# Eight strided loads of 16 partitions for the first keys of a decode attention, instead of one of 16 and one of 112

## The chip, the cores and the metric

The kernel runs on one core of one Trainium2 chip. The metric is the device time of one execution in microseconds (us), the median over the runs; less is better.

## What is computed

One step of grouped-query attention for one sequence. There are 32 query heads with one query row each, and 8 key/value heads of 65536 rows of 128 bf16 numbers, so four query heads share the keys and values of one head. Keys and values together are 268.4 MB, and each is read once.

```python
B, Hq, Hkv, Sq, Sk, D = 1, 32, 8, 1, 65536, 128
k = jnp.repeat(k, Hq // Hkv, axis=1)
v = jnp.repeat(v, Hq // Hkv, axis=1)
scores = jnp.einsum("bhqd,bhkd->bhqk", q, k) * D ** -0.5
p = _softmax(scores, axis=-1)
return jnp.einsum("bhqk,bhkd->bhqd", p, v)
```

## The kernel before

The rows of a head are split in two halves (`pairs`, line 445), which makes 16 rounds (`NR`). In a round each of the 128 partitions holds 256 key rows and 256 value rows of one half, one after another as they lie in memory: 64 KB of keys for each partition, 8 MB for all, and as much of the values. A key row of all partitions together is a tile of 128 x 128. In memory, one partition's run begins 64 KB after that of the partition before.

Each round does this:

- TensorE transposes the key tiles, eight to a PSUM buffer (`pe_transposes`, line 132, the transposes at line 140). VectorE and ScalarE copy the buffers to `ktb` (`evict`, lines 235 and 237). TensorE multiplies the transposed tiles with the four queries (`pe_scores`, line 158).
- VectorE and GpSimd find the maximum, ScalarE takes the exponentials (line 405), and TensorE multiplies them with the values (`stretch`, line 184), which VectorE adds to the running output.

All key and value loads are issued by SP's queue in the order that is written out by hand in `sync_engine` (line 449). Keys lie in `kbuf`, which has room for 256 + 96 tiles, values in `vbuf`, which has room for 256. Loads of the next round wait until the buffers are free (`kfree`, set after the transposes of the first 160 tiles; `vfree` and `vmid`, set by the value products).

The first round's keys come in parts, so that TensorE can begin before all are there: tiles 0 to 63 (`K_PARTS[1]` is 64; 16 KB for each partition, 2 MB), 64 to 159, and 160 to 255 (24 KB for each partition each). The semaphores `krdy[0]` to `krdy[2]` tell that a part has landed, and `pe_transposes` waits for the right one ahead of the first tile of each part. The first part is cut once more, by partitions: 16 rows of partitions, which raise `kfirst` (line 478), and 112, which raise `krdy[0]` (line 479). TensorE waits for `kfirst` before it enters its loop (line 218), and for `krdy[0]` at the loop's first transposes. After the first part come the second and third part (line 462) and the values of the round (line 467), all of which are issued without a wait.

The last round's values come in pieces of 160, 62, 22, 9 and 3 tiles (`V_PIECES` for the last four), so that few products are left when the last one lands.

A DMA raises its semaphore by 16 in all; so seven loads that raise the same semaphore bring it to 7 * 16.

Of the kernel before, what the change touches and what calls it, by code (L numbers as in the profile page):

```python
# [10 lines left out]
P = 128  # L11
# [3 lines left out]
C = 96  # L15
A = 2 * T - C
K_PARTS = (0, 64, A)
# [24 lines left out]
def take(e, sem, n=1):  # L42

    e.wait_ge(sem, n)
    e.sem_inc(sem, -n)  # L45


def bass_standalone__gqa_softmax__decode_kernel(nc, q, k, v, out):
    _, Hq, _, D = q.shape
# [13 lines left out]
    def row_tile(odd, x):  # L63
        return (x + C) % (2 * T) if odd else x
# [6 lines left out]
    def sb(name, shape, dt):  # L71
        return S(nc.sbuf_tensor(name, shape, dt))

    def sem(name):
        return S(nc.semaphore(name))

    kbuf = sb("kbuf", [P, (2 * T + C) * D], DT.bfloat16)
# [38 lines left out]
    krdy = [sem(f"krdy{i}") for i in range(len(K_PARTS))]  # L116
    kfirst = sem("kfirst")
# [47 lines left out]
    def pe_keys(pe, i):  # L165
        for j in range(GA + LAG):
            if j < GA:
                pe_transposes(pe, j, C + j * TB)
            if j >= LAG:
                pe_scores(pe, j - LAG)  # L170
        with pe.If(i % 2 > 0):
            for j in range(GA, G):
                pe_transposes(pe, j, j * TB - A)
        with pe.If(i % 2 < 1):
            for j in range(GA, G):
                pe_transposes(pe, j, C + j * TB)
        for j in range(GA, G):
            pe_scores(pe, j)
# [11 lines left out]
    def pe_values(pe, i):  # L190

        take(pe, vrdy[0], 16)
        take(pe, exd)
        stretch(pe, 1).then_inc(vmid, 1)


        with pe.Fori(i % 2, 2) as s:
            with pe.If(s > 0):  # L200
                take(pe, vrdy[1], 16)
                take(pe, exd)
                stretch(pe, 2).then_inc(pvd, 1)
            with pe.If((i + s) % 2 < 1):
                take(pe, exd)
                stretch(pe, 0).then_inc(pvd, 1)

    def pe_last(pe):
        ins = pe.transpose(fin[0:R, 0:P], acc, identf[:, :])  # L209
        ins.wait_op(t_acc, 1, "sem-ge")  # L210
        ins.then_inc(s_fin, 1)

    def tensor_engine(pe):
        pe.wait_ge(q_sem, 16)
        pe.wait_ge(t_id, 1)
        pe.transpose(trb[0][:, 0:HR], qsb[:, :], ident[0:HR, 0:HR]).then_inc(s_x, 1)  # L216
        pe.wait_ge(t_qT, 1)
        pe.wait_ge(kfirst, 16)
        pe.addr_align(256, offset=LOOP_SLOT, max_nops=16)
        with pe.Fori(0, NR) as i:  # L220
            pe_keys(pe, i)
            pe_values(pe, i)
        pe_last(pe)
# [221 lines left out]
    def pairs(x):  # L445

        return x.rearrange("h (c p t) d -> (h c) p (t d)", c=HALVES, p=P)

    def sync_engine(e):
        kp, vp = pairs(kf), pairs(vf)  # L450

        def cols(a, b):
            return slice(a * D, b * D)

        def load_k(i, odd, split=(0,)):

            for n, f in enumerate(split):
                last = (split + (len(K_PARTS),))[n + 1]
                a, b = K_PARTS[f], (K_PARTS + (2 * T,))[last]
                r = row_tile(odd, a) if b - a < 2 * T else 0  # L460
                t = r if odd else C + r
                e.dma_start(kbuf[:, cols(t, t + b - a)], kp[i][:, cols(r, r + b - a)]).then_inc(krdy[f], 16)
                for x in range(f + 1, last):
                    e.sem_inc(krdy[x], 16)

        def load_v(i, ready, a, b):
            e.dma_start(vbuf[:, cols(a, b)], vp[i][:, cols(a, b)]).then_inc(ready, 16)

        def load_both(i, odd):
            take(e, kfree)  # L470
            load_k(i, odd)
            take(e, vfree)
            load_v(i, vrdy[0], 0, 2 * T)
            e.sem_inc(vrdy[1], 16)


        first = K_PARTS[1] * D
        e.dma_start(kbuf[0:16, C * D:C * D + first], kp[0][0:16, 0:first]).then_inc(kfirst, 16)
        e.dma_start(kbuf[16:P, C * D:C * D + first], kp[0][16:P, 0:first]).then_inc(krdy[0], 16)
        load_k(0, 0, (1, 2))  # L480
        load_v(0, vrdy[0], 0, 2 * T)

        for sm in [vrdy[1]] + vpiece:
            e.sem_inc(sm, 16)

        take(e, kfree)
        load_k(1, 1)
        e.wait_ge(vmid, 1)
        load_v(1, vrdy[0], C, A)
        take(e, vfree)  # L490
        e.sem_inc(vpiece[0], -16)
        load_v(1, vrdy[1], A, 2 * T)
        load_v(1, vpiece[0], 0, C)
        with e.Fori(1, H - 1) as h:
            load_both(2 * h, 0)
            load_both(2 * h + 1, 1)
        i = NR - 2
        take(e, kfree)
        load_k(i, 0, (0, 2))
        take(e, vfree)  # L500
        load_v(i, vrdy[0], 0, A)
        load_v(i, vrdy[1], A, 2 * T)
        i = NR - 1
        take(e, kfree)
        load_k(i, 1, (0, 1, 2))
        take(e, vfree)
        for sm in vpiece:
            e.sem_inc(sm, -16)
        load_v(i, vrdy[0], C, 2 * T)
        e.sem_inc(vrdy[1], 16)  # L510
        r = 0
        for n, sm in zip(V_PIECES, vpiece):
            load_v(i, sm, r, r + n)
            r += n
        ins = e.dma_start(of[HR - R:HR, :], olast[:, :])
        ins.wait_op(t_last, 1, "sem-ge")
        ins.then_inc(o_sem, 16)
        e.wait_ge(o_sem, 32)

    block = S(nc.Block())  # L520
    block.tensor(tensor_engine)
    block.vector(vector_engine)
    block.scalar(scalar_engine)
    block.gpsimd(gpsimd_engine)
    block.sync(sync_engine)
    es.close()

# [26 lines left out]
```

## Time and profile before

| | before |
|---|---|
| median of 3 runs | 633.45 us (633.38 to 633.49) |
| the profiled execution | 633.33 us |
| its span, from the first to the last instruction | 631.3 us |
| mean granted clock of TensorE | 0.77 |
| busy: TensorE, VectorE, ScalarE | 78%, 45%, 37% |
| moved by the DMA engines | 268.59 MB, mean 425 GB/s |

The profile's page divides the span into 40 slices of 15.8 us. A digit of an engine's row is its busy share in tenths; the DMA row has the mean busy share of the core's 16 DMA engines, the row below what they moved. Lines such as `L462` are lines of the kernel's file. A DMA's time to landing is counted from its issue to its semaphore. In rows of a timeline the columns are start, duration, engine, line, operation, output and input, and in brackets the idle time before it with what ended it. SPq is SP's queue of issues; PEq is TensorE's sequencer.

### The profile page before, as it was taken

What the parts mean: (1) busy time and instruction counts of PE and PEld (TensorE: products, weight loads), DVE (VectorE), ACT (ScalarE), POOL (GpSimd) and SP (SyncE); (2) the same over time, 40 slices, a digit from 0 to 9 for tenths busy, and PEclk for the clock granted to TensorE, in tenths of its full rate; (3) what the DMA queues carried; (4) which work ended last, traced back from release to release, by engine and by line L of the source; (5) the groups of instructions that cost most, each with busy time, mean ns of one, the idle gap of its engine ahead of it and who ended that gap; (6) DMA issues with size and microseconds to landing.
All of it is one profiled execution on the core that took longest, in us unless ns stands there. A gap on an engine that the chain in (4) does not pass through costs nothing. (4 is left out here: it accounts for less than half of the span.)

```text
span 631.3 us, 26949 instructions
## 1 busy us (share of the span) xinstructions
PE 489.3 (78%) x12290; PEld 484.8 (77%) x12290; DVE 284.4 (45%) x667; ACT 235.2 (37%) x466; POOL 16.4 (3%) x49
## 2 busy tenths in 40 slices
PE   2763994958959599596986949769596796999887
PEld 2763994958959499595986949769496796989886
DVE  2430562715527155361653616445172452747354
ACT  1330351523516144152442504436052351535343
POOL 0000000000000000000000000000000000000000
PEclk9875795967959587585876958779596785969696
DMA  9999999999999999999999999999999999999997
GB/s 279 446 446 410 415 446 448 419 444 419 444 436 432 432 432 436 432 432 436 432 432 432 432 440 424 444 424 444 424 444 432 436 432 432 412 433 426 432 433 293
DMA packets 6459, 268.59 MB, mean 425 GB/s; under 512 B 818, under 2 KB 946, under 8 KB 1202
## 3 DMA queue, kind: packets, MB, share of 16 engines
q1 hardware_dynamic: 6360, 268.44, 99.1%
q8 instruction: 7, 0.11, 0.1%
q10 hardware_dynamic: 90, 0.02, 0.0%
q14 instruction: 2, 0.02, 0.0%
HBM read 268.44 MB, written 0.01 MB: 425 GB/s over the span
## 5 line engine op out<-in xcount | busy, mean ns | idle before, releaser
L140 PE MATMUL trb<-ident,kbuf 128*128 128x128 bf16 x4096 | 302.2, 236 | 112.2 <-PEq L45 106.3
L140 PEld LDWEIGHTS trb<-ident,kbuf 128*128 128x128 bf16 x4096 | 269.9, 107 | 113.9 <-issue 113.5
L235 ACT ACTIVATE ktb<-trb 128x1024 bf16<-128x1024 bf16 x176 | 180.1, 1023 | 353.9 <-PE trb L140 347.4
L237 DVE COPY ktb<-trb 128x1024 bf16<-128x1024 bf16 x336 | 221.8, 689 | 173.8 <-PE trb L140 171.0
L158 PE MATMUL qkb<-qcur,ktb 128*128 128x4 bf16 x4096 | 132.3, 164 | 0.9 <-issue 0.9
L158 PEld LDWEIGHTS qkb<-qcur,ktb 128*128 128x128 bf16 x4096 | 124.5, 96 | 1.0 <-issue 1.0
L184 PE MATMUL pvb<-pts,vbuf 128*128 128x4 bf16 x2560 | 71.7, 166 | 13.4 <-PEq L45 9.7
L184 PEld LDWEIGHTS pvb<-pts,vbuf 128*128 128x128 bf16 x2560 | 69.9, 102 | 15.2 <-issue 14.8
L405 ACT ACTIVATE pts<-qkb,negm 128x160 bf16<-128x160 f32 (+1 forms) x128 | 51.9, 548 | 0.0
L184 PE MATMUL qkb<-pts,vbuf 128*128 128x4 bf16 x1536 | 43.4, 166 | 7.9 <-PEq L45 7.8
L184 PEld LDWEIGHTS qkb<-pts,vbuf 128*128 128x128 bf16 x1536 | 42.4, 104 | 8.5 <-issue 8.3
L272 DVE TENSOR_REDUCE cmax<-qkb 128x4 f32<-128x640 f32 (+1 forms) x32 | 22.1, 691 | 59.1 <-DVEq L45 59.1
L405 ACT ACTIVATION_READ_ACCUMULATOR pts<-qkb,negm 128x1 f32 x128 | 34.2, 267 | 0.0
L441 POOL PARTITION_ALL_REDUCE cmaxa<-cmax x32 | 12.0, 375 | 580.2 <-POOLq L45 580.2
L322 DVE COPY acc<-qkb 128x4 f32<-128x4 f32 x8 | 1.3, 162 | 40.9 <-DVEq L45 40.9
L399 ACT ACTIVATE alpha<-dm 128x4 f32<-128x4 f32 x32 | 6.4, 201 | 32.5 <-ACTq L45 32.5
L300 DVE TENSOR_TENSOR lp<-lp,alpha 128x4 f32<-128x4 f32 x24 | 3.9, 163 | 26.9 <-DVEq L45 26.9
L311 DVE TENSOR_TENSOR acc<-acc,pvb 128x4 f32<-128x4 f32 x32 | 5.0, 158 | 21.0 <-DVEq L45 20.1
L289 DVE TENSOR_TENSOR m<-m,cmaxa 128x4 f32<-128x4 f32 x24 | 3.8, 159 | 8.8 <-DVEq L45 8.8
L308 DVE TENSOR_TENSOR acc<-acc,alpha 128x4 f32<-128x4 f32 x24 | 3.9, 163 | 4.2 <-DVEq L45 3.7
L216 PE MATMUL trb<-ident,qsb 32*128 32x32 bf16 x1 | 0.2, 204 | 5.5 <-DMA qsb<-in_q_dram 5.5
L216 PEld LDWEIGHTS trb<-ident,qsb 32*128 32x128 bf16 x1 | 0.1, 100 | 5.5 <-DMA qsb<-in_q_dram 5.5
(42 smaller groups left out, 37.6 us busy)
## 6 DMA issues: line engine op xcount, KB each, us to landing
kbuf<-in_k_dram SPq DMA_DIRECT2D x5, 3072.0 KB, 25.2
vbuf<-in_v_dram SPq DMA_DIRECT2D x2, 5120.0 KB, 23.6
vbuf<-in_v_dram SPq DMA_DIRECT2D x3, 3072.0 KB, 20.1
kbuf<-in_k_dram SPq DMA_DIRECT2D x1, 5120.0 KB, 17.8
vbuf<-in_v_dram SPq DMA_DIRECT2D x1, 2048.0 KB, 18.2
kbuf<-in_k_dram SPq DMA_DIRECT2D x1, 2048.0 KB, 18.3
vbuf<-in_v_dram SPq DMA_DIRECT2D x1, 1984.0 KB, 31.3
kbuf<-in_k_dram SPq DMA_DIRECT2D x1, 1792.0 KB, 10.7
```

The costliest lines, as they stand in the source:

```text
L140: ins = pe.transpose(trb[j % NTB][:, i * P:(i + 1) * P], kbuf[:, t * D:(t + 1) * D], ident[:, :])
L158: ins = pe.matmul(bank[:, t * R:(t + 1) * R], lhsT=ktb[:, off:off + P], rhs=qcur[:, :], start=True, stop=True)
L184: ins = pe.matmul(vsum[q], lhsT=vbuf[:, r * D:(r + 1) * D], rhs=pts[:, r * R:(r + 1) * R], start=r == a, stop=r == b - 1)
L235: ins = e.activation(dst, trb[j % NTB][:, :], AF.Copy).then_inc(eva, 1)
L237: ins = e.tensor_copy(dst, trb[j % NTB][:, :]).then_inc(evd, 1)
L272: e.tensor_reduce(cmax[:, :], qkb[part][:, 0:n * R].rearrange("p (t g) -> p g t", g=R), AX.X, ALU.max).then_inc(cm, 1)
L300: chain(e, lambda: e.tensor_tensor(lp[:, :], lp[:, :], alpha[u % 2][:, :], ALU.mult), lambda: e.tensor_tensor(lp[:, :], lp[:, :], rsum[u % ...
L308: return lambda: e.tensor_tensor(acc, acc, alpha[u % 2][:, :], ALU.mult)
L311: return lambda: e.tensor_tensor(acc, acc, vsum[q], ALU.add)
L399: e.activation(alpha[u % 2][:, :], dm[u % 2][:, :], AF.Exp, scale=scale)
L405: ins = e.activation(pv[:, g, r:r + n], sv[:, g, 0:n], AF.Exp, bias=negm[b][:, g:g + 1], scale=scale, accum_out=rsum[b][:, g:g + 1])
L441: e.partition_all_reduce(cmaxa[:, :], cmax[:, :], P, bass.bass_isa.ReduceOp.max).then_inc(cma, 1)
```

## The change

The 128 rows of partitions of the first part were loaded as rows 0 to 15 and rows 16 to 127. Now they are eight loads of 16 rows each, and load p takes the rows p, p + 8, ... p + 120. The first seven raise `kfirst`, the eighth raises `krdy[0]`. TensorE waits for all of the first seven at `kfirst`, where before it waited for one load. The bytes, the source and the destination of each row are the same as before, and the eight loads stand where the two stood, ahead of everything else on SP's queue. The size of each run in memory (16 KB) is the same too. No other instruction of any engine is added, removed or moved.

```diff
@@ tensor_engine
         pe.wait_ge(t_qT, 1)
-        pe.wait_ge(kfirst, 16)
+        pe.wait_ge(kfirst, 7 * 16)
         pe.addr_align(256, offset=LOOP_SLOT, max_nops=16)
         with pe.Fori(0, NR) as i:
             pe_keys(pe, i)
@@ sync_engine
-        first = K_PARTS[1] * D
-        e.dma_start(kbuf[0:16, C * D:C * D + first], kp[0][0:16, 0:first]).then_inc(kfirst, 16)
-        e.dma_start(kbuf[16:P, C * D:C * D + first], kp[0][16:P, 0:first]).then_inc(krdy[0], 16)
+        n = K_PARTS[1]
+        for p in range(8):
+            ins = e.dma_start(kbuf[p:P:8, cols(C, C + n)], kp[0][p:P:8, cols(0, n)])
+            ins.then_inc(kfirst if p < 7 else krdy[0], 16)
         load_k(0, 0, (1, 2))
         load_v(0, vrdy[0], 0, 2 * T)
```

## The prediction

> **What bounds the kernel now.** I read four views in this order: the page's slices and its DMA section, the chain that ended last, the DMA issues with their time to landing, and the first microseconds in stages and in order of time. The page first:
>
> ```profile
> span 631.3 us, 26949 instructions
> PE 489.3 (78%) x12290; PEld 484.8 (77%) x12290; DVE 284.4 (45%) x667; ACT 235.2 (37%) x466; POOL 16.4 (3%) x49
> ...
> DMA  9999999999999999999999999999999999999997
> GB/s 279 446 446 410 415 446 448 419 444 419 444 436 432 432 432 436 432 432 436 432 432 432 432 440 424 444 424 444 424 444 432 436 432 432 412 433 426 432 433 293
> ...
> q1 hardware_dynamic: 6360, 268.44, 99.1%
> ```
>
> No compute engine is above 78%. The DMA engines are busy in every slice, and all slices but the first and the last move 410 to 448 GB/s. So the kernel is one long stream of 268.44 MB on one queue (q1). A stream that never pauses ends earlier only by moving its bytes faster, and the slice that stands out for that is the first, at 279 GB/s. The chain shows whether the end follows the stream:
>
> ```profile
> 621.24 4.52 PE pvb L184 x160
> 625.77 2.45 PE qkb L184 x84
> 628.22 0.01 issue
> 628.23 0.49 PE qkb L184 x12
> ```
>
> These are the last value products. The issues of the loads they wait for, in order of time and by size (KB, then median us from issue to landing), stand here:
>
> ```profile
> 593.97 2.23 SPq L467 DMA_DIRECT2D vbuf<-in_v_dram  x5
> ```
>
> ```profile
> vbuf<-in_v_dram SPq DMA_DIRECT2D x1, 1984.0 KB, 31.3
> vbuf<-in_v_dram SPq DMA_DIRECT2D x1, 704.0 KB, 32.6
> vbuf<-in_v_dram SPq DMA_DIRECT2D x1, 288.0 KB, 32.9
> vbuf<-in_v_dram SPq DMA_DIRECT2D x1, 96.0 KB, 32.6
> ```
>
> Five issues in 2.23 us are 0.45 us each, so the four small ones start near 594.4, 594.9, 595.3 and 595.8 and land near 625.7, 627.5, 628.2 and 628.4. The 84 products begin at 625.77 and the last 12 at 628.23, each just as its piece lands. What delays the whole stream by a microsecond therefore delays the end by a microsecond.
>
> The first microseconds in stages (window and its length, busy time of each engine, TensorE clock, DMA share, GB/s):
>
> ```profile
> 0.00:1.80 1.80, 0.00 (x0) 0.00 (x0) 0.57 (x6) 0.60 (x1) 0.98 (x9) 1.00 0.08 18
> 1.80:4.60 2.80, 0.00 (x0) 0.00 (x0) 1.95 (x12) 0.89 (x2) 0.00 (x0) 1.00 1.09 179
> 4.60:10.20 5.60, 0.20 (x1) 0.10 (x1) 0.59 (x4) 0.00 (x0) 0.00 (x0) 1.00 1.01 281
> 10.20:12.00 1.80, 0.00 (x0) 0.00 (x0) 0.00 (x0) 0.00 (x0) 0.00 (x0) 1.00 1.11 410
> 12.00:620.00 608.00, 481.31 (x12032) 477.35 (x12032) 277.53 (x623) 232.15 (x455) 14.63 (x38) 0.77 1.00 432
> ```
>
> The DMA share is full from 1.8 us on while the rate is not: the engines have work and are slow at it. Full rate is 432 GB/s, which is 27 GB/s on each of the 16 engines. The first part of the keys is 128 rows (partitions) of 16 KB, eight rows for each engine. Call one row on each of the 16 engines, 262 KB together, a turn. At full rate a turn takes 262 / 432 = 0.607 us. Before the change the first turn is the load of 16 rows and seven turns are the load of 112. The window 1.8:4.6 moved 179 x 2.8 = 501 KB, about two turns; the window 4.6:10.2 moved 1574 KB, six turns of 0.93 us. Their loads and landings:
>
> ```profile
> kbuf<-in_k_dram SPq DMA_DIRECT2D x1, 256.0 KB, 4.5
> kbuf<-in_k_dram SPq DMA_DIRECT2D x1, 1792.0 KB, 10.7
> ```
>
> ```profile
> 0.73 0.40 SPq L478 DMA_DIRECT2D kbuf<-in_k_dram  x1
> 1.19 0.41 SPq L479 DMA_DIRECT2D kbuf<-in_k_dram  x1
> 1.65 0.90 SPq L462 DMA_DIRECT2D kbuf<-in_k_dram  x2
> 2.59 0.44 SPq L467 DMA_DIRECT2D vbuf<-in_v_dram  x1
> ```
>
> The 16 rows land at 0.73 + 4.5 = 5.2 us, the 112 rows at 1.19 + 10.7 = 11.9 us.
>
> **The rate of a turn, before and after.** This is the term that decides. The loads of 128 rows run at full rate, so there are 16 ways into the on-chip memory at 27 GB/s each, with eight of the 128 rows behind each. The first turn writes 16 neighbouring rows. Two turns took 2.8 us, and one of the later kind takes 0.93, which leaves 1.9 us, 3.1 times 0.607; since an engine reads ahead of its writes (the third turn is read from 4.6, before the first has landed at 5.2) this is a lower bound, and I take four times, 2.43 us. Four neighbouring rows then share one way, and a way holds two such groups of four. [...]
>
> After the change the rows of a turn are p, p+8, ... p+120. They touch 16 of the 32 groups of four, every second one. Whether these fall on 16 ways once or on 8 ways twice depends on how far apart the two groups of one way lie. Neighbouring groups are excluded, for 16 neighbouring rows would then have only two ways and need 4.9 us. An even distance (4, 8 or 16 groups, as a layout by address bits has it) puts the rows of each turn in pairs, and the turn takes 2 x 0.607 = 1.21 us; an odd distance gives 0.607. The trace of before does not show the distance. Bounds from its rows: 0.607 (loads of 128 rows) and 2.43 us (16 neighbours); the nearest row in spacing is 0.93 (7 apart), but with a step of 8 the collisions repeat in every turn instead of sliding, so I take 1.21.
>
> [...]
>
> **The sum.** The first load's landing is 4.5 us after its issue, of which 2.43 was the turn, so 2.1 us is the way there and back. After the change the last of the eight loads lands at 0.73 + 2.1 + 8 x 1.21 = 12.5 us instead of 11.9: +0.6 us for the first part, and for the whole stream behind it, since every engine writes its first-part rows before anything else.
>
> SP issues eight loads for two, at 0.45 us each. The three bigger loads behind them move from 1.65, 2.1 and 2.59 to about 4.4, 4.9 and 5.3 us. They are needed when the eighth turn is drained, near 11.6 us, or at 1.8 + 8 x 0.607 = 6.7 us at full rate, so the move costs nothing; without that cover it would cost 2.7 us. Each load of 16 rows starts 0.45 us after the last and needs 1.21, so the queue doesn't run dry. Six further completions are bounded below by 0, and above by the tail: loads of 288 and 96 KB landed about 0.7 and 0.2 us after their forerunners, which is their bytes at 432 GB/s. I take 0. [...]
>
> The wait on kfirst now ends with the seventh load, at about 12.5 - 1.2 = 11.3 us instead of 5.2. What is queued behind it on TensorE is the loop's entry and then the wait for the rest of the first part:
>
> ```profile
> 12.04 6.04 PE L140 MATMUL trb<-ident,kbuf 128*128 128x128 bf16 x64 [6.36 <-PEq L45]
> 20.65 0.27 PE L140 MATMUL trb<-ident,kbuf 128*128 128x128 bf16 x1 [2.56 <-PEq L45]
> ```
>
> TensorE began at 12.04 when the 112 rows were in. It will begin near 12.7. It has 1.2 us for the loop's entry, which no row prices; if that took up to 2 us more, the 2.56 us of idle time after the first 64 transposes, spent waiting for the second part, would take it up, and the stream doesn't wait for TensorE there:
>
> ```profile
> 29.77 0.33 SPq L462 DMA_DIRECT2D kbuf<-in_k_dram  x1
> ```
>
> That next issue waits for the keys' buffer. By then 2.8 MB were moved up to 12 us (from the windows) and 17.8 us x 432 GB/s = 7.7 MB after it, of 16.8 MB issued; 6.3 MB, or 14 us, were still queued. So 0.6 us here is free, and only the stream's own delay stays. The profiled execution took 633.33 us, 2.0 beyond its span, and lies 0.12 under the median of 633.45. With +0.6: 633.9 against the profiled execution, 634.1 against the median.
>
> **Rivals.**
>
> [...]
>
> *Faster: collisions don't repeat.* If the distance matters little, or one of a pair gets ahead and they stop meeting, a turn takes the 0.93 us of the 112 rows. Then 0.73 + 2.1 + 7.4 = 10.3 us, 1.6 us earlier: 631.9. For it speaks that this is the nearest measured row, and that the slow first turn, 2.43 us, is gone. [...]
>
> *Much faster: sixteen ways.* With an odd distance all turns run at 0.607: 7.7 us, 4.2 earlier, 629.3. Only the layout speaks against it.
>
> *The wait on kfirst becomes the bound:* it would need more than 1.2 + 2.5 us of loop entry and then 14 us of cushion; I give it nothing.
>
> **How the numbers follow.** A change of 0.2%, 1.27 us, is about what a measurement of this kernel can tell from none. Pairs that share (forecast): 0.62, from +0.4 to +1.7, since a loss of 10% on each turn is easily had; 0.43 of that lies within 1.27 us and 0.19 above. Pairs that cost more: 0.18. Turns of 0.93: 0.13. Full rate: 0.07. So faster 0.20, same 0.43, slower 0.37. The range leaves out the full-rate case and reaches to the middle of the costly pairs: 631.8 to 636.7. The forecast's own range is 633.8 to 635.1.
>
> **What would show it.** In the changed profile: window rates near 218 GB/s from about 2 to 11.5 us; the eighth load landing near 12.5 us; TensorE's first key transposes near 12.7, and its second stop (20.65) and the last value pieces later by the same 0.6; kfirst's move without effect. Rates of 280 or more in that stretch would prove me wrong towards faster, under 200 towards slower. If the first part moves one way and the end another, the step from stream to end is wrong.

## The result: slower by 0.91 us, and the profile after

| | before | after |
|---|---|---|
| median of 22 runs each | 633.36 us | 634.27 us |
| range of the runs | 632.9 to 633.66 | 634.04 to 634.39 |
| ratio, 95% interval | | 1.0015 (1.0008 to 1.0021) |
| the profiled execution, and its span | 633.33, 631.3 | 634.24, 632.4 |

The change costs 0.15% (0.08% to 0.21%). The first microseconds of the changed kernel in stages, cut as they were before the change:

```profile
0.00:1.80 1.80, 0.00 (x0) 0.00 (x0) 0.57 (x6) 0.63 (x1) 0.98 (x9) 1.00 0.01 1
1.80:4.60 2.80, 0.18 (x1) 0.10 (x1) 2.12 (x13) 0.85 (x2) 0.00 (x0) 1.00 1.13 265
4.60:10.20 5.60, 0.00 (x0) 0.00 (x0) 0.42 (x3) 0.00 (x0) 0.00 (x0) 1.00 0.96 202
10.20:12.00 1.80, 0.00 (x0) 0.00 (x0) 0.00 (x0) 0.00 (x0) 0.00 (x0) 1.00 1.17 278
12.00:620.00 608.00, 478.53 (x11963) 474.64 (x11964) 276.15 (x620) 230.12 (x446) 14.63 (x38) 0.77 1.00 432
```

The opening is faster (265 GB/s for 179), which fits that the slow turn of 16 neighbouring rows is gone. The long middle is slower (202 for 281), and from 12 us on both streams run at 432. Cut where six turns begin and end, the middle shows the time of a turn:

```profile
3.90:11.30 7.40, 0.00 (x0) 0.00 (x0) 0.87 (x7) 0.00 (x0) 0.00 (x0) 1.00 1.02 213
```

262 KB at 213 GB/s are 1.23 us. SP's issues and TensorE's work in order of time, after the change:

```profile
0.73 5.04 SPq L479 DMA_DIRECT2D kbuf<-in_k_dram  x8
5.81 1.05 SPq L462 DMA_DIRECT2D kbuf<-in_k_dram  x2
6.91 0.44 SPq L467 DMA_DIRECT2D vbuf<-in_v_dram  x1
...
13.15 6.40 PE L140 MATMUL trb<-ident,kbuf 128*128 128x128 bf16 x64 [9.55 <-PEq L45]
21.77 0.66 PE L140 MATMUL trb<-ident,kbuf 128*128 128x128 bf16 x8 [2.22 <-PEq L45]
```

An issue took 0.63 us and not 0.45, and in the first 1.8 us hardly a byte moved (1 GB/s for 18). TensorE begins at 13.15 instead of 12.04, and its next stop ends at 21.77 instead of 20.65. The chain that ended last:

```profile
622.39 4.48 PE pvb L184 x160
626.87 0.03 issue
626.90 2.96 PE qkb L184 x96
```

The last value products begin at 626.90 instead of 625.77. So 1.1 us are lost before the first transpose, and it stays 1.1 us to the end. The whole executions differ by 0.91, a little less, as what lies outside the span differs by 0.2 between these two.

### The profile page after: what moved, and what is told of

It is laid out like the page before. It is cut to its first block, busy times and chain, and to the rows that moved or that the text cites. A ratio compares the mean times of both kernels' runs of the same rounds, so it can differ in the third digit from the quotient of the medians.

```text
span 632.4 us, 26955 instructions
## 1 busy us (share of the span) xinstructions
PE 488.4 (77%) x12290; PEld 483.8 (76%) x12290; DVE 284.1 (45%) x667; ACT 235.2 (37%) x466; POOL 16.4 (3%) x49
## 5 line engine op out<-in xcount | busy, mean ns | idle before, releaser
L290 DVE TENSOR_TENSOR dm<-m 128x4 f32<-128x4 f32 x24 | 3.9, 163 | 0.8
L301 DVE TENSOR_TENSOR lp<-lp,rsum 128x4 f32<-128x4 f32 x24 | 3.9, 162 | 0.8
```

Source lines behind the costliest of these rows:

```text
L290: lambda: e.tensor_tensor(dm[u % 2][:, :], mo[:, :], mn[:, :], ALU.subtract),
```

## Experiments

Each kernel below is the changed one with one more edit, timed beside the kernel before on the same chip. Three dots mark lines of an edit or a view that are left out; where an edit changes the number of loads, the count that TensorE waits for at `kfirst` follows it. For each, three rows are shown: the rate in a window inside the first part (its length, engine busy times, clock, DMA share, GB/s), and, from the timeline, TensorE's first key transposes and its last 96 value products.

**One load of 128 rows.**

```diff
-        pe.wait_ge(kfirst, 7 * 16)
...
-        for p in range(8):
-            ins = e.dma_start(kbuf[p:P:8, cols(C, C + n)], kp[0][p:P:8, cols(0, n)])
-            ins.then_inc(kfirst if p < 7 else krdy[0], 16)
+        e.dma_start(kbuf[:, cols(C, C + n)], kp[0][:, cols(0, n)]).then_inc(krdy[0], 16)
```

> The first part as one load of 128 rows that raises krdy[0]; the wait on kfirst is left out, since nothing raises it. Theory of the ways (16 ways into the on-chip memory, rows that are written in the same turn on the same way share it): each engine has a way to itself, a turn takes 0.61 us, the part lands near 7.2 us instead of 11.9 (before) or 13.0 (after), and the end follows: 628.5 to 629.5 us. Rival A (the start of the stream is slow whatever the rows are, since queues and memory have to come up to speed): turns of 0.9 us and more, landing after 10 us, 631.5 us or more. Rival B (the stream is not what sets the end): landing early, time within 0.3 us of 633.4.

```profile
3.50:7.10 3.60, 0.20 (x1) 0.10 (x1) 1.25 (x9) 0.00 (x0) 0.00 (x0) 1.00 0.99 425
...
8.37 6.37 PE L140 MATMUL trb<-ident,kbuf 128*128 128x128 bf16 x64 [2.94 <-PEq L45]
...
622.14 2.93 PE L184 MATMUL qkb<-pts,vbuf 128*128 128x4 bf16 x96
```

629.54 us, 0.9942 of the kernel before (0.9929 to 0.9956). Full rate from the third turn on, 0.62 us each. So the slow turns were not a matter of coming up to speed: rival A falls, and so does B, for the end moved with the landing. A slow start of its own remains: in the first 3.6 us this kernel moved no more than the changed one (147 and 148 GB/s on average). The part came about 1 us later than expected (8.2 for 7.2), and the time lies just above the forecast range.

**Eight loads by columns.** Each has all 128 rows and eight of the 64 tiles.

```diff
+        n = K_PARTS[1] // 8
...
+            a = p * n
+            ins = e.dma_start(kbuf[:, cols(C + a, C + a + n)], kp[0][:, cols(a, a + n)])
```

> Eight loads again, 256 KB each, but each has all 128 rows and an eighth of their columns (2 KB for each row). Theory of the ways: no sharing, so as fast as one load of 128 rows but for the pace of the issues (0.45 to 0.63 us each for 0.61 us of bytes): landing at 7 to 8 us, 628.5 to 630 us. Rival C (what costs is that there are eight loads, by their issue, their completions or their fixed price): landing at 12 us or later, 634 us or more.

```profile
3.50:8.00 4.50, 0.11 (x1) 0.00 (x0) 1.25 (x9) 0.00 (x0) 0.00 (x0) 1.00 0.93 288
...
9.99 5.84 PE L140 MATMUL trb<-ident,kbuf 128*128 128x128 bf16 x64 [6.39 <-PEq L45]
...
624.11 2.92 PE L184 MATMUL qkb<-pts,vbuf 128*128 128x4 bf16 x96
```

630.93 us, 0.9964 (0.9951 to 0.9978): a miss by 0.9 us at the slow end, and far from rival C. Eight loads of the same 256 KB beat the kernel before. They cost 1.4 us over one load (630.93 for 629.54; in the profiled executions TensorE begins at 9.99 for 8.37); whether that is the number of loads or the rows of 2 KB isn't separated here.

**Stride of 4 in one half of the rows.**

```diff
+            a, b = p // 4 * 64 + p % 4, p // 4 * 64 + 64
+            ins = e.dma_start(kbuf[a:b:4, cols(C, C + n)], kp[0][a:b:4, cols(0, n)])
```

> Eight loads of 16 rows with a stride of 4 inside one half of the rows (0, 4, ... 60 and so on, then 64, 68, ... 124 and so on): 16 neighbouring groups of four rows. If the two groups of one way lie 8 groups (32 rows) apart, the 16 rows of a load meet in pairs on 8 ways as with the stride of 8: turns of 1.26 us, landing near 13.0, 634.0 to 634.6 us. If they lie 16 groups (64 rows) apart, each row has its own way: 0.61 us, landing near 7.5, 628.5 to 629.5 us. If they lie 4 groups apart, four rows meet: about 20 us and 642 us.

```profile
3.80:11.10 7.30, 0.00 (x0) 0.00 (x0) 0.97 (x8) 0.00 (x0) 0.00 (x0) 1.00 1.01 219
...
12.82 5.46 PE L140 MATMUL trb<-ident,kbuf 128*128 128x128 bf16 x64 [9.22 <-PEq L45]
...
626.51 2.92 PE L184 MATMUL qkb<-pts,vbuf 128*128 128x4 bf16 x96
```

633.91 us, 1.0011 (1.0002 to 1.002), 0.1 us under the forecast range. Turns of 1.20 us: rows 0 to 60 in steps of four meet in pairs. That rules out a distance of 64 rows (0.61 us). It doesn't rule out 16 rows, where the expectation is wrong: with two groups of four on a way, those 16 groups would meet in pairs too, and not four at a time. The 32 neighbouring rows further down decide that: paired at 16 rows they would reach four ways and need some 2.4 us a turn (four times 0.607), and they need 1.23. So of the three distances 32 rows are left.

**Sixteen neighbouring rows, eight times.**

```diff
+            a, b = 16 * p, 16 * p + 16
+            ins = e.dma_start(kbuf[a:b, cols(C, C + n)], kp[0][a:b, cols(0, n)])
```

> Eight loads of 16 neighbouring rows: 0 to 15, 16 to 31, and so on. Theory of the ways: four rows on each of four ways in every turn, 2.43 us to 2.6 us each, so the part lands at 21.5 to 23.5 us and the time is 643 to 645 us. Rival C (eight loads cost what eight loads cost, whichever rows): 634.3 us as after the change. Rival B (the stream does not set the end): within 0.3 us of 634.3.

```profile
4.70:17.00 12.30, 0.20 (x1) 0.10 (x1) 0.60 (x4) 0.00 (x0) 0.00 (x0) 1.00 1.02 128
...
19.54 5.98 PE L140 MATMUL trb<-ident,kbuf 128*128 128x128 bf16 x64 [13.48 <-PEq L45]
...
633.20 2.93 PE L184 MATMUL qkb<-pts,vbuf 128*128 128x4 bf16 x96
```

641.35 us, 1.0131 (1.0115 to 1.0146). The number of loads and their size are those of the change; which rows go together costs 7 us more, and rivals B and C fall. But a turn takes 2.05 us and not 2.43, so the time falls short of the forecast range. The next pair of experiments bears on why.

**Another order of the same loads.** The changed kernel once more, and the same with the order 0, 4, 1, 5, 2, 6, 3, 7.

```diff
-        for p in range(8):
+        for i in range(8):
+            p = i // 2 + i % 2 * 4
...
-            ins.then_inc(kfirst if p < 7 else krdy[0], 16)
+            ins.then_inc(kfirst if i < 7 else krdy[0], 16)
```

> The changed kernel once more, as the yardstick for the three kernels beside it: first part landed near 13.0 us, 634.0 to 634.6 us.

> The same eight strided loads in the order 0, 4, 1, 5, 2, 6, 3, 7, so that each turn uses the other eight ways than the turn before it. In step (both engines of a pair always on the same way together): nothing changes, turns of 1.26 us, landing 12.8 to 13.2 us, 634.0 to 634.6 us. With a lead (an engine that is ahead of its partner has the next way to itself until the partner comes, so each turn is shorter by the lead; in the order 0 to 7 that can happen at one turn only, the fifth): turns of 0.9 to 1.15 us, landing 10 to 12.2 us, 631.4 to 633.6 us. If the number of strided loads or their issue were what costs, the order would not matter: 634.0 to 634.6 us.

The reordered kernel:

```profile
3.80:10.20 6.40, 0.00 (x0) 0.00 (x0) 0.97 (x8) 0.00 (x0) 0.00 (x0) 1.00 1.01 246
...
12.01 5.94 PE L140 MATMUL trb<-ident,kbuf 128*128 128x128 bf16 x64 [8.41 <-PEq L45]
...
625.72 2.92 PE L184 MATMUL qkb<-pts,vbuf 128*128 128x4 bf16 x96
```

The yardstick repeated at 634.20 us (1.0014, 1.0005 to 1.0023), the reordered kernel took 633.13 (0.9998, 0.9989 to 1.0007). Nothing but the order differs, and 1.07 us are gone, about as much as the whole loss of the change: a turn takes 262 / 246 = 1.07 us. The number of loads, their size and the pace of their issue (eight in 5.04 us) are the same in both, so none of them makes this difference. Partners in step would take the same time in both orders. That an engine gains by its lead when the next turn uses other ways is the theory that forecast this; how large the leads are no row shows. By that theory the ways change at each turn in the sixteen neighbouring rows too, which fits the 2.05 us, but wasn't tried apart from it.

**Fewer loads with a step.** Four loads of 32 rows with a stride of 4, and two of 64 with a stride of 2. These are the lines that issue the loads.

```diff
+        for p in range(4):
+            ins = e.dma_start(kbuf[p:P:4, cols(C, C + n)], kp[0][p:P:4, cols(0, n)])
```

```diff
+        for p in range(2):
+            ins = e.dma_start(kbuf[p:P:2, cols(C, C + n)], kp[0][p:P:2, cols(0, n)])
```

> [...] In step: 634.0 to 634.6 us. With a lead: as the changed order of loads, or up to 0.3 us earlier for the earlier first byte: 631.2 to 633.6 us. If the number of loads cost: half of what eight cost over one load of 128 rows, near 632 us, with turns that are still 1.26 us.

> [...] Theory of the ways: landing 11.5 to 12.9 us, 633 to 634.4 us, though there are only two loads. If the number of loads cost: as one load of 128 rows or a little more, 629.5 to 630.5 us. If the stride itself delays the first byte (2.1 us in place of 1.8), it does so here too, with an issue of 0.6 us and more.

First the four loads, then the two:

```profile
3.90:7.80 3.90, 0.00 (x0) 0.00 (x0) 0.88 (x7) 0.00 (x0) 0.00 (x0) 1.00 1.02 397
...
9.24 5.99 PE L140 MATMUL trb<-ident,kbuf 128*128 128x128 bf16 x64 [5.64 <-PEq L45]
...
623.13 2.92 PE L184 MATMUL qkb<-pts,vbuf 128*128 128x4 bf16 x96
```

```profile
3.80:7.40 3.60, 0.00 (x0) 0.00 (x0) 0.96 (x8) 0.00 (x0) 0.00 (x0) 1.00 1.03 437
...
8.39 6.44 PE L140 MATMUL trb<-ident,kbuf 128*128 128x128 bf16 x64 [4.79 <-PEq L45]
...
622.11 2.98 PE L184 MATMUL qkb<-pts,vbuf 128*128 128x4 bf16 x96
```

630.82 us (0.9962, 0.9948 to 0.9975) and 629.86 us (0.9947, 0.9933 to 0.9961). Both forecasts of the theory of the ways fell: turns of 0.66 and 0.60 us where 1.2 was forecast for partners in step. They follow if each engine takes consecutive rows of a load, which puts rows 8 apart into a turn. The four loads would then write the same rows turn by turn as the reordered eight loads, which took 1.07 us. The two loads came out in the range of the rival that the number of loads costs; the four are 1.2 us faster than that rival has them. At this point two readings were open: the engines are dealt the rows in another way, so that a load that reaches all 16 ways gives one to each engine; or what decides is the number of rows in a load, or of loads.

**The same number of loads without a step.** Four loads of 32 neighbouring rows, whose edit is shown, and two of 64 in the same way.

```diff
+            a, b = 32 * p, 32 * p + 32
+            ins = e.dma_start(kbuf[a:b, cols(C, C + n)], kp[0][a:b, cols(0, n)])
```

> Four loads of 32 neighbouring rows (0 to 31, 32 to 63, and so on), beside the four loads of 32 rows with a stride of 4 that ran turns of 0.61 us and landed at 9.1 us. Number and size of the loads are the same, and the step between rows is 1 and not 4. Theory of the ways: 32 neighbouring rows reach 8 of the 16 ways, so two engines meet on each: turns of 1.05 to 1.26 us, landing 10.7 to 12.6 us, 632 to 634 us. If the number of rows in a load decides (16 are slow, 32 are not): turns of 0.61 us, landing 8.5 to 9.1 us, 630 to 631 us. With a step of 1 the issue should be back at 0.45 us and the first byte at 1.8.

> Two loads of 64 neighbouring rows, beside the two loads of 64 rows with a stride of 2 that landed at 8.3 us. Theory of the ways: 64 neighbouring rows reach no more than the 8 ways that 32 reach, since rows 32 apart share one: turns of 1.2 to 1.26 us, landing 11.5 to 12.6 us, 632.7 to 634 us. If the number of rows or of loads decides: 0.61 us, landing near 8.2 us, 629.5 to 630.2 us.

First the four loads, then the two:

```profile
3.60:11.00 7.40, 0.20 (x1) 0.10 (x1) 1.15 (x9) 0.00 (x0) 0.00 (x0) 1.00 1.02 213
...
13.14 5.29 PE L140 MATMUL trb<-ident,kbuf 128*128 128x128 bf16 x64 [6.88 <-PEq L45]
...
626.83 2.92 PE L184 MATMUL qkb<-pts,vbuf 128*128 128x4 bf16 x96
```

```profile
4.10:11.60 7.50, 0.00 (x0) 0.00 (x0) 0.70 (x6) 0.00 (x0) 0.00 (x0) 1.00 1.00 210
...
13.55 5.20 PE L140 MATMUL trb<-ident,kbuf 128*128 128x128 bf16 x64 [9.95 <-PEq L45]
...
627.20 2.98 PE L184 MATMUL qkb<-pts,vbuf 128*128 128x4 bf16 x96
```

634.38 us (1.0018, 1.0009 to 1.0028) and 634.74 us (1.0024, 1.0015 to 1.0034), some 0.4 to 0.7 us above the forecast ranges. Turns of 1.23 and 1.25 us, with as many rows and loads as the two kernels of 0.66 and 0.60. So neither the number of rows in a load nor that of loads decides; which rows go together does, and pairs at 32 rows account for all four kernels. 64 neighbouring rows are no faster than 32 (1.25 us a turn for 1.23), as the theory of the ways forecast.

What no run separates is where the ways lie. Row r of every load here goes to partition r and comes from r x 64 KB further on in memory, so a way into the on-chip memory and a way out of the memory that holds the keys would look alike. That there are 16 of them (432 GB/s over 16 engines, and loads of 128 rows at that rate), and that they lead into the on-chip memory, is argued, not shown.

**The load of the queries moved.** In these traces the slow issues of 0.6 us went together with an early landing of the queries (1.6 to 1.8 us after their issue; with the fast issues 4.4 to 5.3, and 2.4 in the eight loads by columns), so the queries' load, on ACT's queue, was issued 0.45 us later: in the changed kernel, and in that of two loads of 64 rows.

```diff
-        e.dma_start(qsb[:, :], qf).then_inc(q_sem, 16)
         e.wait_ge(t_z, 1)
+        e.dma_start(qsb[:, :], qf).then_inc(q_sem, 16)
```

> The changed kernel, with the load of the queries on ACT's queue moved behind ACT's wait for GpSimd's memsets (about 0.5 us later), so that it doesn't start together with SP's first load. In the kernels so far the first byte of the keys came at 2.1 us, the queries landed 1.6 to 1.8 us after their issue and SP needed 0.6 us for each issue, or the first byte came at 1.8, the queries landed after 4.4 to 5.3 us and SP needed 0.45 us; never a mixture but for one (2.4 us). Theory of the race (which of the two queues is served first): SP is first now, issues of 0.45 us, first byte at 1.8, first part landed near 12.75 us, 633.7 to 634.1 us. Rival (the strided or bigger form of the load is what is slow to issue): issues of 0.6 us, first byte at 2.1, landed at 13.0 us, 634.0 to 634.5 us.

> The two loads of 64 rows with a stride of 2, with the load of the queries moved in the same way. Theory of the race: first byte at 1.8, the first part landed at 7.7 to 8.2 us, 629.4 to 629.8 us, at best a little faster than one load of 128 rows. Rival: as without the move, landed at 8.3 us, 629.7 to 630.1 us. If the queries come late instead, behind the keys' first packets, TensorE's first transposes start later than the landing and the time is the same.

SP's issues in the first of the two:

```profile
0.73 5.04 SPq L479 DMA_DIRECT2D kbuf<-in_k_dram  x8
```

634.33 us (1.0015, 1.0006 to 1.0024) and 629.85 us (0.9942, 0.9928 to 0.9955): no change in either. Issues stay at 0.63 us. The race falls: in the first of the two the queries land 3.5 us after their issue for 1.6 in the changed kernel, and the slow issue is there all the same.

## Why the prediction was right, and where it was not

*The bound.* From the first transposes to the last 96 products there are 625.77 - 12.04 = 613.73 us before and 613.75 after. In the kernels of the experiments it is 613.65 to 613.89 us, but for the eight loads by columns (614.12). The first part landed anywhere between 8.2 and 19.4 us, and the end followed by the same amount, to within 0.4 us. TensorE isn't what passes the delay on, for it still stands idle for 2.22 us after its first 64 transposes (2.56 before).

*The rate of a turn.* Forecast 1.21 us, measured 1.23 over the last six. The pairing was argued from "an even distance", which the author assumed, as no row of before showed it; that it comes of a layout by address bits no run shows. The stride of 4 and the 32 neighbouring rows together settle the distance at 32 rows (1.20 and 1.23 us a turn). The 218 GB/s that the prediction looks for stand in no run: 262 KB in 1.21 us are 217 GB/s, and 213 were measured.

*The landing.* Forecast 12.5 us; measured near 13.0, and TensorE starts 0.1 to 0.2 us after a landing. Eight slightly longer turns are 0.2 us of that. The rest lies in "2.1 us is the way there and back". It was what a turn of 2.43 us leaves of the first load's 4.5, and 2.43 was taken as four times 0.607. In the kernel of sixteen neighbouring rows the first load lands after about 4.5 us too (worked out from the median of its eight, 10.1 us, with turns of 2.05 us and issues 0.45 apart), which leaves 2.45. With that the landing is 0.73 + 2.45 + 8 x 1.23 = 13.0 us. The issues were mis-sized as well, 0.63 us for 0.45, and the first bytes came about 0.3 us later than before the change (at 2.1 us for nearly 1.8). But that this delayed the landing isn't shown. The four loads of 32 neighbouring rows have the fast issue and the early bytes:

```profile
0.74 1.79 SPq L480 DMA_DIRECT2D kbuf<-in_k_dram  x4
0.00:1.80 1.80, 0.00 (x0) 0.00 (x0) 0.57 (x6) 0.60 (x1) 0.98 (x9) 1.00 0.14 27
```

That is 0.45 us for an issue, and 27 GB/s in the first 1.8 us where the change has 1. By 3.6 us both kernels have moved the same 0.53 MB (147 and 148 GB/s), and TensorE starts at 13.14 us there and at 13.15 after the change.

*The time.* The landing moved by 1.1 us where 0.6 was forecast, and the time by 0.91, since what lies outside the span is 0.2 us shorter in the changed execution. Nobody forecast that; by so much the nearness to the forecast is luck.

*What was to cost nothing.* The wait on kfirst: TensorE started 0.1 to 0.2 us after the landing in both kernels, and with the wait left out (one load) too. The later issues at L462 and L467: the stream kept 432 GB/s behind the first part. Both as argued.

*The rivals.* A turn of 1.54 us, by which the upper end of the range (636.7) and the chance of 0.18 go, no run shows; the changed kernel has 1.23. Nor does a run show that the turns of the 112 rows hold rows 7 apart and that collisions slide there: how those rows are dealt to the engines, and what makes their turns take 0.93 us, wasn't tried. The choice of 1.21 came out without it. Turns of 0.93: refuted for this order, but its mechanism, one of a pair getting ahead, is what the other order of the loads fits (1.07). Sixteen ways at once was the right picture of the prize, though not of this change: one load of 128 rows, or two of 64 with a stride of 2, have it, and are 3.7 and 3.4 us (0.6% and 0.5%) faster than the kernel before.

## What to carry to other kernels

When a stream of loads sets the time, look for stretches where the DMA share is full and the rate is not, and there try first which rows go together in a load. Here all 128 rows or every second ran at full rate (425 and 437 GB/s) and every fourth near it (397); 16 rows with a stride of 8, or 32 or 64 neighbours, got half (210 to 213), and 16 neighbours 128 GB/s. The number of loads comes second, and what it costs by itself wasn't separated: with rows that run at or near full rate, four loads, whose step is 4 and not 2, took 1.0 us longer than two (630.82 for 629.86), and eight by columns, whose rows are shorter too, 1.4 longer than one. A split of a first load that is meant to start the work early has to be priced by that rate first: here one plain load is the faster start.

## What was not expected of the hardware

- A load of 32 or 64 rows with a step that reaches all ways moves at 397 and 437 GB/s, which speaks against its rows being dealt to the engines in consecutive runs: with those, two engines in step would meet on each way, at about 213, and even the reordered eight loads, which would write the same rows turn by turn as the four, came to 246. How the rows are dealt no trace shows.
- The order of equal loads is worth 1.07 us (633.13 for 634.20).
- An issue of the first part's loads takes 0.40 to 0.47 us in some kernels and 0.60 to 0.63 in others: the slow ones had a step, or 64 neighbouring rows, as their loads. The issues right behind them, which are the same in all these kernels, took longer as well after the change (two in 1.05 us, in 0.90 before), but also behind the fast issues of the eight loads by columns (1.17). Issuing the queries' load 0.45 us later changed nothing; the cause stays open.
